# The opening of a fused Fourier and gated-cosine kernel: a first step without seed, two stores moved, and constant products around the second stage

## The chip, the cores and the metric

The kernel runs on one core of a Trainium2 chip. Five engines work side by side: PE (TensorE, matrix products), DVE (VectorE), ACT (ScalarE), POOL (GpSimd) and SP (SyncE), which here issues the transfers. The metric is device time of one execution in microseconds, the median over the runs shown. Everything is float32.

## The reference

```python
def _attn_ref(x):                       # x: (8, 3008, 256)
    X = np.fft.fft(x, axis=1)
    X = np.fft.fft(X, axis=2)
    return X.real.astype(np.float32)
...
def _moe_ref(x, w_in, w_out):           # (24064, 256), (256, 2048), (2048, 256)
    h = x @ w_in
    g = h * np.cos(h)
    return (g @ w_out).astype(np.float32)
```

The real part of a two-dimensional Fourier transform is fed, row by row, into two products with h times cos(h) between them.

## The kernel before, in words

The Fourier transform along the 256 columns is folded into `w_in`: `fold_weights` (L349) multiplies `w_in` by cosines and sines and gives WC and WS, in four quarters of 512 columns. `take_wn` (L362) takes the first row of a quarter of WS out into the columns of `wn`, and POOL then clears that row, because the row belongs to a column of another symmetry. The transform along the 3008 rows has two stages, 47 times 64. In the first (`fold` L210, `first_half` L231) VectorE or POOL folds a chunk of x, PE multiplies it by a table into `pz`, and ScalarE copies it to `zs`. There are eight chunks for a batch. `store_z` (L266) writes a chunk's `zs` to DRAM and `load_z` (L278) reads it back in another order as `z2`. Both can do a part of the columns, 0 to 4 of 24 or 4 to 24. The second stage (`second_half` L290) multiplies four blocks of `z2` by the table BJ into `pb`, and ScalarE copies the result to `pq`: one group of up to 256 columns, 225 in group 0. There are 6 groups in each of 8 batches.

A group passes through 8 steps of the network, 384 steps in all. A step fills a bank `H` with a seed (`seed` L418, ScalarE: 0.25 plus one row `nb` times a column of `wn`), adds products with WC (`mm1` with 0, L432), copies twice that to `ew` (`act_e`), adds products with WS (`mm1` with 1), and takes `h` as the difference on VectorE (`dve_h`). So one pair of products serves two mirrored sets of rows. Then follow rounding, sine, and the combinations for the second product (`mm2` L507, into banks `M`, seven products instead of eight). `nb` is one row of `pq` spread over 128 partitions: for the first group by a product with a row of ones into `pn` (L317 to L321), for the others by a trip through DRAM (L323 to L325).

The order of the program is written by hand, and every engine runs its own instructions in that order; all transfers are issued by SP in order. Ahead of the steps stands the opening (L640 to L696): first `keep_busy` (L392), products of a constant tile VX that nobody reads; then the eight chunks of batch 0 interleaved with three quarters of the weights; the small parts of the stores (columns 0 to 4) before the first read of z (L681); `fold_quarter(2)`, two constant products (L684); then the last weights, the other parts of the stores of chunks 4 to 7, further constants, the second read of z, and `second_half(0, 0)`. The rest of chunks 2 and 3 is stored ahead of the first read (L674, L675). Then comes `seed(steps[0])` (L721) and the loop over steps (L722), in which step 0 is followed at once by `fold_weights(1, 3)`. The dictionary `opening` (L697) places what is left over into steps 0 to 22, such as `fold_weights(0, 3)`, `take_wn(3)`, VectorE's sums of `w_out` (`combine_w2` L406) and the other groups of batch 0. Steps 3 and later of each batch carry the first stage of the next one, in which POOL folds.

The banks of PSUM are shared: `H` has three, `M` four, and the second stage one.

Of the kernel before, what the change touches and what calls it, by code (L numbers as in the profile page):

```python
# [11 lines left out]
FP = mybir.dt.float32  # L12
# [69 lines left out]
def _width(g):  # L82
    return 225 if g == 0 else 256
# [24 lines left out]
def kernel(  # L108
# [7 lines left out]
    nc = tc.nc  # L116
# [10 lines left out]
    cpool = ctx.enter_context(tc.tile_pool(name="consts", bufs=1))  # L127
# [50 lines left out]
    def load_bj(c0, c1):  # L178
        nc.sync.dma_start(out=BJ[:, c0:c1], in_=B_dr.ap()[:, c0:c1])
# [21 lines left out]
    def psum(name, tag="fft"):  # L201
        return ppool.tile([128, 512], FP, tag=tag, bufs=bank[tag], name=name)
# [63 lines left out]
    def store_z(b, c, j0=0, j1=NJ):  # L266
        half, q = divmod(c, NCH // 2)
        if q == 0 and j0 == 0:
            zds[b, half] = dpool.tile([32, 2 * NJ * 128], FP, tag="zd", bufs=4, name="zd")
        zd, zs = zds[b, half], zss[b, c]  # L270
        for e in range(2):
            p0 = 16 * e + IP * q
            nc.sync.dma_start(
                out=zd[p0 : p0 + IP, 256 * j0 : 256 * j1].rearrange("i (y d) -> y i d", d=128),
                in_=zs[64 * e + 2 * j0 : 64 * e + 2 * j1, :].rearrange("y (i d) -> y i d", d=128),
            )
# [11 lines left out]
    ready = {}  # L288

    def second_half(b, g):  # L290

        T = _width(g)
        z2 = z2s[b]
        pb = psum("pb")
        for q in range(4):
            jj = 4 * g + q
            nc.tensor.matmul(  # L297
                pb[:, 128 * q : 128 * q + 128],
                lhsT=z2[:, jj * 128 : jj * 128 + 128],
                rhs=BJ[:, jj * 128 : jj * 128 + 128],  # L300
                start=True,
                stop=True,
            )
        pq = spool.tile([128, 512], FP, tag="pq", bufs=8, name="pq")
        pv = pq[:, 0 : 2 * T].rearrange("d (e t) -> d e t", e=2)
        bv = pb.rearrange("d (q e k) -> d e q k", q=4, e=2)
        if g == 0:
            nc.scalar.copy(
                out=pv[:, :, 0:192].rearrange("d e (q k) -> d e q k", k=64), in_=bv[:, :, 1:4, :]
            )  # L310
            nc.scalar.copy(out=pv[:, :, 192:225], in_=bv[:, :, 0, 0:33])
        else:
            nc.scalar.copy(out=pv.rearrange("d e (q k) -> d e q k", k=64), in_=bv)
        nb = spool.tile([128, 256], FP, tag="nb", bufs=8, name="nb")
        ready[b, g] = (pq, nb)
        if b == 0 and g == 0:
            pn = psum("pn", "M")  # L317
            nc.tensor.matmul(
                pn[:, 0:T], lhsT=ones, rhs=pq[0:1, T : 2 * T], start=True, stop=True
            )  # L320
            nc.scalar.copy(out=nb[:, 0:T], in_=pn[:, 0:T])  # L321
            return
        nd = dpool.tile([1, 256], FP, tag="nd", bufs=4, name="nd")  # L323
        nc.sync.dma_start(out=nd[:, 0:T], in_=pq[0:1, T : 2 * T])
        nc.sync.dma_start(out=nb[:, 0:T], in_=nd[0:1, 0:T].to_broadcast([128, T]))  # L325


    def transform(b):
        todo = {}
# [19 lines left out]
    def fold_weights(e, n, tag="M"):  # L349
        W = WS if e else WC  # L350
        pw = psum("pw", tag)
        for i in range(2):
            nc.tensor.matmul(  # L353
                pw,
                lhsT=CS[i][:, 128 * e : 128 * e + 128],
                rhs=wr[n // 2][i][:, 512 * (n % 2) : 512 * (n % 2) + 512],
                start=(i == 0),
                stop=(i == 1),
            )
        nc.scalar.copy(out=W[:, 512 * n : 512 * n + 512], in_=pw)  # L360

    def take_wn(n):  # L362
        row = WS[0:1, 512 * n : 512 * n + 512]
        pw = psum("pw", "M")
        for k in range(4):
            nc.tensor.matmul(
                pw[:, k : k + 1],
                lhsT=row[:, 128 * k : 128 * k + 128],
                rhs=ones[:, 0:1],
                start=True,  # L370
                stop=True,
            )
        nc.scalar.copy(out=wn[:, 4 * n : 4 * n + 4], in_=pw[:, 0:4])
        nc.gpsimd.memset(row, 0.0)

    def fold_quarter(n):
        fold_weights(1, n)
        fold_weights(0, n)
        take_wn(n)
# [6 lines left out]
    ones = cpool.tile([1, 128], FP, tag="ones", name="ones")  # L386
    nc.vector.memset(VX[:, 0:512], 1.0)
    nc.vector.memset(ones, 1.0)
    scratch = cpool.tile([1, 128], FP, tag="scratch", name="scratch")
    nc.scalar.activation(out=scratch, in_=ones, func=AF.Sin, bias=0.0, scale=SIN_SCALE / 8)  # L390

    def keep_busy(k, tag, n):  # L392
        pd = psum("pd", tag)
        for i in range(k):
            nc.tensor.matmul(
                pd[:, 0:n],
                lhsT=VX[:, 0:128],
                rhs=VX[:, 0:n],
                start=i == 0,
                stop=i == k - 1,  # L400
            )
# [16 lines left out]
    def seed(s):  # L418
        T = s.T
        s.pq, s.nb = ready[s.b, s.grp]  # L420
        s.H = psum("H", "H")
        for u in range(2):
            f = 2 * s.fp + u
            nc.scalar.activation(  # L424
                out=s.H[:, u * T : u * T + T],
                in_=s.nb[:, 0:T],
                func=AF.Copy,
                bias=0.25,
                scale=wn[:, f : f + 1],
            )  # L430

    def mm1(s, e):  # L432
        T = s.T
        W = WS if e else WC
        for u in range(2):
            f = 2 * s.fp + u
            nc.tensor.matmul(  # L437
                s.H[:, u * T : u * T + T],
                lhsT=W[:, 128 * f : 128 * f + 128],
                rhs=s.pq[:, e * T : e * T + T],  # L440
                start=False,
                stop=True,
                skip_group_check=True,
            )

    def act_e(s):
        s.ew = spool.tile([128, 512], FP, tag="ew", bufs=2, name="ew")
        nc.scalar.mul(out=s.ew[:, 0 : 2 * s.T], in_=s.H[:, 0 : 2 * s.T], mul=2.0)  # L448
# [187 lines left out]
    def chunk(c):  # L636
        fold(0, c, 0)
        fold(0, c, 1)
# [32 lines left out]
    first_half(0, 5)  # L671
    store_z(0, 4, 0, 4)
    store_z(0, 5, 0, 4)
    store_z(0, 2, 4)  # L674
    store_z(0, 3, 4)  # L675
    chunk(7)
    first_half(0, 6)
    first_half(0, 7)
# [2 lines left out]
    for half in range(2):  # L681
        load_z(0, half, 0, 4)
    fold_quarter(2)
    keep_busy(2, "M", 256)  # L684
    load_w(3)
    load_w2(0, 2)
    load_w2(2, 4)
    for c in range(4, 8):
        store_z(0, c, 4)
    load_bj(512, 1024)  # L690
    for half in range(2):
# [1 line left out]
    load_w2(4, 6)  # L693
    load_w2(6, 8)
    load_bj(1024, NJ * 128)
    second_half(0, 0)  # L696
    opening = {  # L697
        0: ((fold_weights, 0, 3), (take_wn, 3), (combine_w2, 0, 2)),
        1: ((combine_w2, 2, 4),),
# [7 lines left out]
    steps = []  # L707
    for b in range(NB):
        for g in range(NG):
            for fp in range(8):  # L710
                s = Step()
# [3 lines left out]
    n = len(steps)  # L715

    def step(t, last=None):
        s = steps[t] if 0 <= t < n else None
        return s if s is not None and (last is None or s.fp == 7) else None

    seed(steps[0])  # L721
    for t in range(n + LAG + 1):  # L722
        cur, prev, old, done = step(t), step(t - 1), step(t - 2), step(t - LAG)
        if cur:
            if t % per == 0:
                todo = transform(cur.b + 1) if cur.b + 1 < NB else {}
            mm1(cur, 0)
            act_e(cur)
            if t == 0:
                fold_weights(1, 3)  # L730
        if t - LAG - 1 == n - 1:
            combine_last(steps[n - 1])
            break
        if step(t - LAG - 1, True):
            take_m(step(t - LAG - 1), 1)
            combine_m(step(t - LAG - 1))
        if done:
            mm2(done, 0)
        if old:
            dve_g(old, 0)  # L740
            dve_g(old, 1)
        if step(t + 1):
            seed(step(t + 1))
        if prev:
            dve_frac(prev, 0)
        if old:
            dve_s(old, 0)
        if prev:
            dve_frac(prev, 1)
            act_sin(prev)  # L750
        if old:
            dve_s(old, 1)
        if step(t - LAG, True):
            take_m(done, 0)
        if cur:
            mm1(cur, 1)
        if done:
            mm2(done, 1)
        if cur:
            dve_h(cur)  # L760
            act_round(cur, 0)
            act_round(cur, 1)
        if old:
            dve_s(old, 2)
        if step(t - LAG - 2, True):
            store_out(step(t - LAG - 2), 0)
        if step(t - LAG - 3, True):
            store_out(step(t - LAG - 3), 1)
        for call in opening.pop(t, ()):
            call[0](*call[1:])  # L770
        for call in todo.pop(t % per, ()):
            call[0](*call[1:])
# [30 lines left out]
```

## Time and profile before

| what | value |
|---|---|
| median of three runs | 1977.77 us |
| the three runs | 1979.92, 1977.70, 1977.77 us |
| profiled execution, own time | 1979.79 us |
| its span, first to last instruction | 1978.0 us |
| mean granted TensorE clock | 0.996 |
| transfers | 88.63 MB, mean 45 GB/s |

The page of the profile gives busy time by engine, the chain that ended last, and the costliest groups of instructions. A row of the timeline has start, length, engine, line, operation, output and inputs, and in brackets the idle time before it with what ended that. PEld is the loading of weights for PE. A float32 product shows as two matmul instructions. The granted clock is a share of full speed.

### The profile page before, as it was taken

Reading aid. Unit: us, or ns where it says so; the run is one execution under the profiler, and the core shown is the slowest. Engines: PE = TensorE matmul, PEld = TensorE weight load, DVE = VectorE, ACT = ScalarE, POOL = GpSimd, SP = SyncE. Lnnn points to the kernel's source line nnn. Section 1 sums busy time; section 2 is a strip of 40 time slices with the busy share of each in tenths; the row PEclk is TensorE's granted clock in tenths of the full one; section 3 lists DMA queues with packets and bytes.
Section 4 is the critical chain, followed back from the end, with each engine's and each line's share of the span. In section 5 each row is a group of like instructions: output and inputs, shape, how many; then the busy total and the mean of one; then the engine's idle time right before and its main releaser. Section 6 shows DMA issues by size and latency. Waiting matters only on the chain.

```text
span 1978.0 us, 28633 instructions
## 1 busy us (share of the span) xinstructions
PE 1953.2 (99%) x9350; PEld 1704.2 (86%) x9350; DVE 1854.5 (94%) x3208; ACT 1483.8 (75%) x2688; POOL 465.4 (24%) x428
## 2 busy tenths in 40 slices
PE   8999999999999999999999999999999999999998
PEld 4888899888988889888898888988889888898887
DVE  2999989999899998999989999999999999899998
ACT  3777777777777778777877777777777777778775
POOL 1132212331133211323122222123311223112111
PEclk8999999999999999999999999999999999999999
DMA  8423121131112212122122311222022220200000
GB/s 199 91 43 58 31 52 37 35 64 35 43 31 42 57 35 43 36 49 50 32 42 42 67 26 36 44 55 55 19 41 51 47 51 20 47 21 10 18 16 22
DMA packets 176682, 88.63 MB, mean 45 GB/s; under 512 B 103303, under 2 KB 173622, under 8 KB 174902
## 3 DMA queue, kind: packets, MB, share of 16 engines
q1 hardware_dynamic: 176374, 86.68, 21.3%
q8 instruction: 75, 1.23, 0.3%
q14 instruction: 73, 0.60, 0.1%
q10 hardware_dynamic: 160, 0.13, 0.0%
HBM read 49.50 MB, written 37.27 MB: 44 GB/s over the span
## 4 chain that ended last, share of the span: by engine, by line
PE 91%; DVE 5%; ACT 1%; issue 1%; DMA 1%; SPq 0%; POOL 0%; DVEq 0%; ACTq 0%; POOLq 0%
PE M L529 53%; PE H L437 31%; PE pz L244 3%; PE pb L297 2%; DVE r L482 1%; DVE S L500 1%; DVE S L493 1%; PE pw L353 1%; DVE S L502 1%; DVE h L453 1%; DVE r L472 1%; ACT r L468 0%; DMA out_dram<-ob 0%; SPq L631 0%; DVE ob L621 0%
## 5 line engine op out<-in xcount | busy, mean ns | idle before, releaser
L478 ACT ACTIVATE r<-r 128x1024 f32<-128x1024 f32 (+1 forms) x384 | 398.5, 1038 | 306.4 <-DVE r L472 305.5
L529 PE MATMUL M<-S,VX 128*128 128x256 f32 (+1 forms) x2304 | 612.6, 375 | 0.0
L529 PEld LDWEIGHTS M<-S,VX 128*128 128x128 f32 x2304 | 438.1, 190 | 50.0
L437 PE MATMUL H<-pq,WS 128*128 128x256 f32 (+1 forms) x1536 | 390.5, 377 | 10.3 <-ACT ew L448 10.0
L437 PE MATMUL H<-pq,WC 128*128 128x256 f32 (+1 forms) x1536 | 395.0, 380 | 1.9 <-ACT H L424 1.9
L529 PE MATMUL M<-r,w 128*128 128x256 f32 (+1 forms) x1536 | 388.5, 375 | 0.0
L424 ACT ACTIVATE H<-nb,wn 128x256 f32<-128x256 f32 (+1 forms) x768 | 364.0, 474 | 17.3 <-DVE r L482 4.7
L453 DVE TENSOR_TENSOR h<-ew,H 128x512 f32<-128x512 f32 (+1 forms) x384 | 257.2, 670 | 98.1 <-PE H L437 89.3
L437 PEld LDWEIGHTS H<-pq,WS 128*128 128x128 f32 x1536 | 289.6, 190 | 53.5 <-ACT ew L448 18.9
L529 PEld LDWEIGHTS M<-r,w 128*128 128x128 f32 x1536 | 301.2, 197 | 27.2
L472 DVE SCALAR_TENSOR_TENSOR r<-r,h 128x512 f32<-128x512 f32 (+1 forms) x384 | 310.1, 808 | 0.0
L437 PEld LDWEIGHTS H<-pq,WC 128*128 128x128 f32 x1536 | 283.7, 190 | 30.7 <-ACT H L424 2.8
L218 POOL TENSOR_TENSOR xf<-xp 94x508 f32<-94x508 f32 x112 | 165.3, 1495 | 566.3 <-PE pz L251 553.8
L493 DVE TENSOR_TENSOR S<-r 128x512 f32<-128x512 f32 (+1 forms) x384 | 291.4, 759 | 0.1
L482 DVE SCALAR_TENSOR_TENSOR r<-h,r 128x512 f32<-128x512 f32 (+1 forms) x384 | 274.2, 714 | 0.0
L468 ACT ACTIVATE r<-H 128x512 f32<-128x512 f32 (+1 forms) x384 | 223.2, 581 | 56.0 <-DVE h L453 53.3
L448 ACT ACTIVATE ew<-H 128x512 f32<-128x512 f32 (+1 forms) x384 | 225.5, 587 | 48.7 <-PE H L437 44.4
L472 DVE SCALAR_TENSOR_TENSOR r<-r,H 128x512 f32<-128x512 f32 (+1 forms) x384 | 255.7, 666 | 0.0
L482 DVE SCALAR_TENSOR_TENSOR r<-H,r 128x512 f32<-128x512 f32 (+1 forms) x384 | 254.5, 663 | 0.3 <-ACT r L478 0.3
L468 ACT ACTIVATE r<-h 128x512 f32<-128x512 f32 (+1 forms) x384 | 236.1, 615 | 0.0
L529 PE MATMUL M<-r,VX 128*128 128x256 f32 (+1 forms) x768 | 225.5, 375 | 0.0
L529 PE MATMUL M<-S,w 128*128 128x256 f32 (+1 forms) x768 | 225.2, 375 | 0.0
(68 smaller groups left out, 1499.7 us busy)
## 6 DMA issues: line engine op xcount, KB each, us to landing
out_dram<-ob SPq DMA_DIRECT2D x728, 32.0 KB
xp<-in_x_dram SPq DMA_DIRECT2D x56, 256.0 KB
zd<-zs SPq DMA_DIRECT2D x112, 96.0 KB
z<-zd SPq DMA_DIRECT2D x28, 384.0 KB
xp<-in_x_dram SPq DMA_DIRECT2D x56, 120.0 KB
nb<-nd SPq DMA_DIRECT2D x40, 128.0 KB
wr<-in_moe_w_in_dram SPq DMA_DIRECT2D x8, 256.0 KB
w<-in_moe_w_out_dram SPq DMA_DIRECT2D x4, 512.0 KB
```

What stands on the lines that cost most here:

```text
L218: (nc.gpsimd if b else nc.vector).tensor_tensor(out=fv[:, e, :, 1:128], in0=xv[:, :, 1:128], in1=xv[:, :, 255:128:-1], op=ALU.subtract if ...
L244: nc.tensor.matmul(pz[rows, a:512], lhsT=w, rhs=fv[:, e, a:512], start=True, stop=True)
L424: nc.scalar.activation(out=s.H[:, u * T : u * T + T], in_=s.nb[:, 0:T], func=AF.Copy, bias=0.25, scale=wn[:, f : f + 1],)
L437: nc.tensor.matmul(s.H[:, u * T : u * T + T], lhsT=W[:, 128 * f : 128 * f + 128], rhs=s.pq[:, e * T : e * T + T], start=False, stop=True, ...
L448: nc.scalar.mul(out=s.ew[:, 0 : 2 * s.T], in_=s.H[:, 0 : 2 * s.T], mul=2.0)
L453: nc.vector.tensor_tensor(out=s.h[:, 0 : 2 * T].rearrange("p (u t) -> p u t", u=2)[:, :, ::-1], in0=s.ew[:, 0 : 2 * T].rearrange("p (u t) ...
L468: nc.scalar.activation(out=r, in_=h, func=AF.Copy, bias=BIG, scale=1.0)
L472: nc.vector.scalar_tensor_tensor(out=r, in0=r, scalar=-BIG, in1=h, op0=ALU.add, op1=ALU.subtract)
L478: nc.scalar.activation(out=r, in_=r, func=AF.Sin, bias=0.0, scale=SIN_SCALE)
L482: nc.vector.scalar_tensor_tensor(out=r, in0=h, scalar=-0.25, in1=r, op0=ALU.add, op1=ALU.mult)
L493: nc.vector.tensor_tensor(out=sv[:, 0:2], in0=gv[:, 2:3].to_broadcast([128, 2, T]), in1=gv[:, 0:4:3], op=ALU.subtract,)
L529: nc.tensor.matmul(acc[key][m // 2][:, 256 * (m % 2) : 256 * (m % 2) + T], lhsT=w, rhs=a, start=first, stop=s.fp == 7, skip_group_check=True,)
```

## The change

The first step gets no seed from ScalarE. Its bank is filled with 0.25 by VectorE ahead of the second stage, and the row's part is added by two products with one row each (`seed_first`): the row of `wn` as it stood in WS, kept in a new tile `wrow`, times the row of `pq`. The row `nb`, still needed from step 1 on, is spread behind the first products and their copy (`spread_nb`). The rest of chunks 2 and 3 is stored behind the first read of z, ahead of that of chunks 4 to 7. One more constant product stands before the second stage (three, not two), and two stand behind it.

```diff
@@ second_half, first group of batch 0
-            pn = psum("pn", "M")
-            nc.tensor.matmul(
-                pn[:, 0:T], lhsT=ones, rhs=pq[0:1, T : 2 * T], start=True, stop=True
-            )
-            nc.scalar.copy(out=nb[:, 0:T], in_=pn[:, 0:T])
             return
...
+    def spread_nb():
+        pq, nb = ready[0, 0]
+        T = _width(0)
+        pn = psum("pn", "M")
+        nc.tensor.matmul(pn[:, 0:T], lhsT=ones, rhs=pq[0:1, T : 2 * T], start=True, stop=True)
+        nc.scalar.copy(out=nb[:, 0:T], in_=pn[:, 0:T])
@@ take_wn
         nc.scalar.copy(out=wn[:, 4 * n : 4 * n + 4], in_=pw[:, 0:4])
+        if n == 0:
+            nc.scalar.copy(out=wrow, in_=row[:, 0:256])
         nc.gpsimd.memset(row, 0.0)
...
+    wrow = cpool.tile([1, 256], FP, tag="wrow", name="wrow")
...
+    def seed_first(s):
+        for u in range(2):
+            nc.tensor.matmul(
+                s.H[:, u * s.T : u * s.T + s.T],
+                lhsT=wrow[:, 128 * u : 128 * u + 128],
+                rhs=s.pq[0:1, s.T : 2 * s.T],
+                start=False,
+                stop=True,
+                skip_group_check=True,
+            )
@@ the opening
     store_z(0, 5, 0, 4)
-    store_z(0, 2, 4)
-    store_z(0, 3, 4)
     chunk(7)
...
     fold_quarter(2)
-    keep_busy(2, "M", 256)
+    keep_busy(3, "M", 256)
     load_w(3)
     load_w2(0, 2)
     load_w2(2, 4)
-    for c in range(4, 8):
+    for c in range(2, 8):
         store_z(0, c, 4)
...
-    second_half(0, 0)
     opening = {
...
-    seed(steps[0])
+    first = steps[0]
+    first.H = psum("H", "H")
+    nc.vector.memset(first.H[:, 0 : 2 * first.T], 0.25)
+    second_half(0, 0)
+    keep_busy(2, "M", 256)
+    first.pq, first.nb = ready[0, 0]
     for t in range(n + LAG + 1):
...
             mm1(cur, 0)
+            if t == 0:
+                seed_first(cur)
             act_e(cur)
             if t == 0:
+                spread_nb()
                 fold_weights(1, 3)
```

## The prediction

> **What bounds the kernel now.** I read the page first, then the chain of waits in the window where the work changes, then the granted clock there, and last the timeline of single engines.
>
> ```profile
> span 1978.0 us, 28633 instructions
> PE 1953.2 (99%) x9350; PEld 1704.2 (86%) x9350; DVE 1854.5 (94%) x3208; ACT 1483.8 (75%) x2688; POOL 465.4 (24%) x428
> PE 91%; DVE 5%; ACT 1%; issue 1%; DMA 1%; SPq 0%; POOL 0%; DVEq 0%; ACTq 0%; POOLq 0%
> ```
>
> PE is busy for 1953.2 of 1978.0 us and holds 91% of the chain. The change touches no instruction of the 384 steps but the first. It can only shift the time at which the steps start, so the question is how many us the opening loses and whether the rest follows. The chain through the opening:
>
> ```profile
> 34.47 2.03 DMA z<-zd
> ...
> 36.64 1.63 PE pb L297 x8
> 38.30 0.49 ACT pq L308
> 38.81 0.23 ACT pq L311
> 39.08 1.13 PE pn L318 x2
> 40.23 0.36 ACT nb L321
> 40.61 0.46 ACT H L424
> 41.09 0.46 ACT H L424
> 41.60 1.87 PE H L437 x4
> 43.47 3.41 PE pw L353 x4
> 46.88 1.06 PE H L437 x4
> 47.94 1.72 PE pw L353 x4
> ```
>
> Columns are start, length, what. The reader is to see two things. From 39.08 to 41.60 nothing but the spreading of one row (pn, nb) and the seeds of step 0 is on the path. And four products of L353 take 3.41 us at 43.47 but 1.72 at 47.94. The second is the clock, in the table of windows (after the busy times come the granted clock, the DMA share and GB/s):
>
> ```profile
> 36.00:37.00 1.00, 0.36 (x3) 0.39 (x4) 0.00 (x0) 0.00 (x0) 0.00 (x0) 1.00 0.73 101
> 37.00:38.00 1.00, 1.00 (x7) 0.96 (x6) 0.00 (x0) 0.00 (x0) 0.00 (x0) 0.56 0.81 277
> ...
> 40.00:41.00 1.00, 0.19 (x1) 0.00 (x0) 0.00 (x0) 0.74 (x2) 0.00 (x0) 0.50 1.06 365
> 41.00:42.00 1.00, 0.40 (x1) 0.41 (x2) 0.00 (x0) 0.51 (x2) 0.00 (x0) 0.50 0.80 265
> ```
>
> The clock is halved in the 37th us, right behind PE's gap ahead of pb, and by the lengths of L353 it is full again shortly before 47.94.
>
> Does a shift reach the end? Behind the opening VectorE is the bound for some 50 us, then PE:
>
> ```profile
> 48.04 0.62 DVE L453 TENSOR_TENSOR h<-ew,H 128x450 f32<-128x450 f32 x1 [19.40 <-PE H L437]
> 80.00:100.00 20.00, 19.38 (x106) 17.48 (x105) 20.00 (x36) 15.83 (x31) 3.71 (x5) 1.00 0.14 24
> 100.00:120.00 20.00, 20.00 (x98) 17.15 (x97) 19.79 (x33) 14.98 (x29) 7.77 (x7) 1.00 0.15 34
> ```
>
> VectorE is full from 80 to 100, PE from 100 on; both regimes begin with VectorE's first h, at 48.04, which waited for PE. If that moves and no transfer is late for it, the end moves by as much.
>
> **The change part by part.** I follow the path to that first h.
>
> *Start of the second stage.* It needs z and a free PE. The stores:
>
> ```profile
> 29.75 0.27 SPq L273 DMA_DIRECT2D zd<-zs x1
> 30.91 0.40 SPq L273 DMA_DIRECT2D zd<-zs x1
> 32.48 0.31 SPq L273 DMA_DIRECT2D zd<-zs x1
> 29.87 0.59 ACT L260 COPY zs<-pz 128x512 f32<-128x512 f32 x1 [0.61 <-PE pz L251]
> 34.37 1.13 PE L395 MATMUL pd<-VX 128*128 128x256 f32 x4
> 36.64 1.62 PE L297 MATMUL pb<-BJ,z 128*128 128x128 f32 x8 [1.14 <-DMA z<-zd]
> ```
>
> By their place in the program, the four issues from 29.75 to 30.91 are the moved stores; the stores of chunks 6 and 7 follow, the last at 32.48. Without the four, chunk 6 goes at 29.75, and chunk 7 when its copy ends (29.87 + 0.59 = 30.46), its last issue at about 30.9. The last read of z then goes at 34.47 - 1.6 = 32.9 and z is there at 34.9 instead of 36.5. But the third constant product is now in front: two pairs took 1.13, and a third adds half of that without the fill. L353's row below gives 3.70 / 8 = 0.46 for one 512-column pass, so two 256-column passes add 0.46. PE is free at 34.37 + 1.13 + 0.46 = 35.96, so about 1 us of the earlier z is not used. pb starts at 35.9 (I let it overlap the drain), **0.75** sooner.
>
> *Clock.* With that product and two more behind pb, PE has no gap above some 0.1 us from 29.76 on, so I take it at full clock through the opening. Rows at full clock:
>
> ```profile
> 29.76 3.70 PE L353 MATMUL pw<-wr,CS 128*128 128x512 f32 x8
> 71.98 1.05 PE L297 MATMUL pb<-BJ,z 128*128 128x128 f32 x8
> 62.98 0.92 PE L437 MATMUL H<-pq,WC 128*128 128x225 f32 x4
> 63.74 0.93 PE L529 MATMUL M<-r,w 128*128 128x225 f32 x4
> ```
>
> pb ends at 35.9 + 1.05 = 36.95 (now 38.27). Next on PE came 39.08 - 38.27 = 0.81 after pb, for the two copies of pq; that gives 37.76. The two new constant products last 1.13 less a drain, about 0.9, so to 37.85: they hide beside the copies and cost 0.1. At half clock they would need 1.8 and cost 1.0.
>
> *Removed:* pn, nb and two seeds ahead of the first products: 41.60 - 39.08 = **2.52**.
>
> *Added on PE:* the first products at full clock pass in 0.76 (62.98 to 63.74, start to start), the one-row products have as many columns and passes. No row shows them; bounds are 0.76 (same spacing) and 1.13 (two pn at full clock, 1.13 / 2 each, not overlapped). I take 0.76, as they are queued back to back. The spreading of the row (pn) now stands in front of L353: half of 0.76, 0.38 (bound 0.57). Then L353 1.72 and the second products 0.92.
>
> **Sum:** 37.85 + 0.76 + 0.76 + 0.38 + 1.72 + 0.92 = 42.39, against 47.94 now (46.88 + 1.06): **5.55 us earlier**. The clock's part is pb 0.58, pn 0.57, first products 0.95, L353 1.69, second 0.14: 3.9. The other 1.65 is order.
>
> *Costed at nothing.* The constant fill of H, on VectorE, falls in its 19.40 us of idleness. The copy of wrow (like nb, 0.36) makes POOL's clearing of that row 0.4 us later, near 16.3, and with it POOL's next fold copy and perhaps the chunk after it; the bound is 0.5 us, and a wait for x further on covers it:
>
> ```profile
> 26.99 1.81 PE L244 MATMUL pz<-xf,L 128*64 128x512 f32 x5 [1.38 <-POOL xf L225]
> 54.02 0.33 SPq L149 DMA_DIRECT2D xp<-in_x_dram x1
> SPq L149 <- DMA z<-zd: 1.5, 1, 1.5
> 58.00:60.00 2.00, 2.00 (x6) 1.78 (x6) 2.00 (x6) 1.84 (x4) 0.00 (x0) 0.50 1.03 194
> 62.51 0.62 DVE L453 TENSOR_TENSOR h<-ew,H 128x450 f32<-128x450 f32 x1 [0.26 <-PE M L529]
> ```
>
> Step 1's seeds need nb; ScalarE makes it at 40 and the seeds after L353's copy near 42, ahead of their products at 44.8. *The moved stores* sit on SP ahead of the constants' and z's second load. That z landed by 54.0 (SP's wait for it ended there) and is first used at 71.98, 66.4 after the change: four issues of up to 0.75 us, less the 1.6 us earlier start, leave 10 us of room. The weights behind the first z come 1.6 us sooner: their fast stretch ends near 41.2 (365 GB/s, then 265), 39.6 after, the half of w2 for VectorE's sums at 42.9 earlier still.
>
> *The second fall of the clock* (58 to 60) stays, as the gaps around it move along. It cost VectorE 0.26 us. [...]
>
> The profiled execution took 1979.79 us (span 1978.0): 1979.79 - 5.55 = **1974.2**. The runs shown lie at two levels, 1977.70 and 1977.77, and 1979.92; the profiled one is of the upper. I take the 2.1 us between them as clock: full rather than half speed for 4 us more in the opening. A kernel with no low stretch has one level, and 1974.2 stands for it: 3.6 under the median (0.18%), 5.6 under the upper level.
>
> [...]
>
> **The rivals.**
>
> *The levels are not the opening's clock* (0.18). Then all 5.55 comes off the median: 1972.2. For it: nothing profiled shows a run of the lower level. Against: no other place of this trace has a low clock for long.
>
> *The clock falls anyway* (0.13), through products that don't count as activity or gaps elsewhere (the one-column products just before 34.37 are nearly idle). Only the 1.65 of order is left: 1977.77 - 1.65 = 1976.1. For it: products stood back to back from 41.60, and L353 from 43.47 to 46.88 was still slow: the clock rises late. Against: it need not rise here, only stay, and the constant products are full passes as L353's, under which it stood at 1.00.
>
> *z is not earlier* (0.07): the stores of chunks 6 and 7 or the read land at 36.5 for another reason than the queue. pb starts at 36.64, 0.75 is lost: 1975.0.
>
> *Slower: the clock is low before the constant products start* (0.08). Place: PE from 34.4 on. Three products take 2.5 and end at 37.1, pb 1.63 (38.75), two products 1.8 (40.5), first and one-row products 1.5 each (43.5), pn 0.75, L353 3.41, second products 1.5 (49.2), L353 3.41 again, 52.6 against 49.66 now: 2.9 later, 1982.7. It decides if the clock falls by 34.4, before the last product of the weights is done; what speaks for it is PE's 1.38 us wait at 26.99, against it the clock of 1.00 until 37.
>
> **How the numbers follow.** Forecast 1974.2 with chance 0.54, spread 1973.3 to 1975.2 by the bounds above (one-row products and pn up to 0.56 dearer, second fall -0.26 to +0.75, pb's start 0.3). About 0.2% of 1977.77, 3.96 us, is what a measurement of this kernel can tell from no change; that is 1973.8. Of the forecast 0.24 lies beyond it and 0.30 within. Faster: 0.24 + 0.18 = 0.42. Same: 0.30 + 0.13 + 0.07 = 0.50. Slower: 0.08. The range 1972.2 to 1976.2 takes in all but the slower rival and part of the edges.
>
> **What would show it.** Right: granted clock 1.00 from 29 to about 46; pb starting near 35.9 straight behind pd; mm1 (L437) of step 0 near 37.9; h near 42.5; PE's next steps 5.5 us earlier to the end. Wrong: a clock of 0.50 before 46, pb waiting for z, VectorE's L414 waiting for w2, PE waiting for z at the second pb, or a first h at 42.5 with a later loss (VectorE beside POOL's folds, or a longer second fall).

## The result, and the profile after

The changed kernel took 1974.46 us (median of 13 runs, 1973.65 to 1975.57), against 1979.83 for the kernel before in as many (1977.70 to 1981.32). The ratio is 0.9975, with a 95% interval from 0.9968 to 0.9983: 0.25% faster. That is clear of no change, but not quite of the 0.2% that the prediction called the limit of what can be told, since the interval reaches down to 0.17%. The forecast time was 1974.2. What it had too low is the kernel before: its three runs had a median of 1977.77, thirteen have 1979.83.

The page of the changed kernel answers to the lines shown of before. Its profiled execution took 1974.87 us.

```profile
span 1973.1 us, 28657 instructions
PE 1948.9 (99%) x9360; PEld 1702.4 (86%) x9360; DVE 1854.4 (94%) x3209; ACT 1482.7 (75%) x2687; POOL 465.1 (24%) x428
PE 91%; DVE 5%; DMA 2%; ACT 1%; issue 1%; SPq 0%; DVEq 0%; POOL 0%; ACTq 0%; POOLq 0%
```

The span is 4.9 us shorter, with nearly the same work on every engine. (PE has ten matmul instructions more, and its busy time still falls by 4.3 us, since those of the opening run at full clock.) The chain of waits through the opening, start, length, what; L400 is `keep_busy`, L453 `mm1`, L439 the one-row products, L355 `fold_weights`:

```profile
35.20 1.49 PE pd L400 x6
36.69 0.89 PE pb L297 x8
37.59 0.86 PE pd L400 x4
38.45 0.98 PE H L453 x4
39.43 0.95 PE H L439 x4
40.38 0.38 PE pn L327 x2
40.76 1.91 PE pw L355 x4
42.68 0.76 PE H L453 x4
```

Where the chain of before went from SP over a transfer to PE, and from there twice to ScalarE and back, it now stays on PE. No wait for z is left in it. The same table of windows as before, with the granted clock third from the end:

```profile
37.00:38.00 1.00, 1.00 (x9) 0.95 (x8) 0.00 (x0) 0.38 (x1) 0.00 (x0) 1.00 0.90 254
40.00:41.00 1.00, 1.00 (x6) 0.70 (x5) 0.00 (x0) 0.58 (x2) 0.00 (x0) 1.00 1.02 355
46.00:47.00 1.00, 1.00 (x6) 0.72 (x5) 0.71 (x2) 0.16 (x1) 0.51 (x1) 1.00 0.94 323
```

It is 1.00 where it was 0.50. Two more rows of VectorE's timeline set the measure for everything below: the fold of chunk 6, which waits for the last fourth of x, and the first h.

```profile
26.92 1.28 DVE L218 TENSOR_TENSOR xf<-xp 94x508 f32<-94x508 f32 x2 [0.92 <-DMA xp<-in_x_dram]
43.55 0.62 DVE L469 TENSOR_TENSOR h<-ew,H 128x450 f32<-128x450 f32 x1 [13.62 <-PE H L453]
```

In the kernel before that fold began earlier, and the first h later (48.04, shown with the prediction):

```profile
26.16 2.48 DVE L218 TENSOR_TENSOR xf<-xp 94x508 f32<-94x508 f32 x4 [1.74 <-DMA wr<-in_moe_w_in_dram]
```

The bracket of this row names a load of weights, as brackets are inferred. The semaphores of the trace show the last load of x itself: it landed at 26.04, and at 26.80 in the changed kernel. In all ten profiles of the table below that landing lies 0.12 to 0.13 us ahead of the fold, whatever the bracket names.

So x arrived 0.76 us later in the profiled execution of the changed kernel, and the first h still came 4.49 us sooner. From the fold to the first h it is 21.88 us before and 16.63 after: 5.25 us gained, with x's arrival taken out.

### The profile page after: what moved, and what is told of

The parts are those of the page before. It is cut to its first block, busy times and chain, and to the rows that moved or that the text cites. A ratio compares the mean times of both kernels' runs of the same rounds, so it can differ in the third digit from the quotient of the medians.

```text
span 1973.1 us, 28657 instructions
## 1 busy us (share of the span) xinstructions
PE 1948.9 (99%) x9360; PEld 1702.4 (86%) x9360; DVE 1854.4 (94%) x3209; ACT 1482.7 (75%) x2687; POOL 465.1 (24%) x428
## 4 chain that ended last, share of the span: by engine, by line
PE 91%; DVE 5%; DMA 2%; ACT 1%; issue 1%; SPq 0%; DVEq 0%; POOL 0%; ACTq 0%; POOLq 0%
PE M L545 53%; PE H L453 31%; PE pz L244 3%; PE pb L297 2%; DVE r L498 1%; DMA xp<-in_x_dram 1%; DVE S L516 1%; DVE S L509 1%; DVE S L518 1%; DVE h L469 1%; DVE r L488 1%; ACT r L484 0%; PE pw L355 0%; DMA out_dram<-ob 0%; SPq L647 0%
## 5 line engine op out<-in xcount | busy, mean ns | idle before, releaser
L453 PE MATMUL H<-pq,WS 128*128 128x256 f32 (+1 forms) x1536 | 390.2, 376 | 11.5 <-ACT ew L464 11.2
L453 PE MATMUL H<-pq,WC 128*128 128x256 f32 (+1 forms) x1536 | 393.9, 379 | 0.5 <-ACT H L429 0.5
L453 PEld LDWEIGHTS H<-pq,WS 128*128 128x128 f32 x1536 | 289.3, 190 | 53.9 <-ACT ew L464 20.0
L453 PEld LDWEIGHTS H<-pq,WC 128*128 128x128 f32 x1536 | 283.2, 190 | 28.9 <-ACT H L429 0.8
```

The source lines that it names most:

```text
L453: nc.tensor.matmul(s.H[:, u * T : u * T + T], lhsT=W[:, 128 * f : 128 * f + 128], rhs=s.pq[:, e * T : e * T + T], start=False, stop=True, ...
```

## The experiments

Twelve runs were made, in four sets of kernels on one chip each; the kernel before ran beside each set (medians 1979.44, 1979.13, 1978.95 and 1979.20). One table holds what the profiles of the first two sets have in common, beside those of before and of the changed kernel: the start of chunk 6's fold, the start of pb in the timeline, the first h, the difference of fold and h, and what is left from the first h to the end of that execution's own time.

| kernel | fold | pb | first h | fold to h | own time | h to end | median |
|---|---|---|---|---|---|---|---|
| before | 26.16 | 36.64 | 48.04 | 21.88 | 1979.79 | 1931.75 | 1979.83 |
| changed | 26.92 | 36.53 | 43.55 | 16.63 | 1974.87 | 1931.32 | 1974.46 |
| products only (e1) | 26.52 | 38.26 | 48.24 | 21.72 | 1979.20 | 1930.96 | 1976.61 |
| no products (e2) | 26.72 | 36.82 | 48.50 | 21.78 | 1979.33 | 1930.83 | 1977.74 |
| none behind (e3) | 27.68 | 37.63 | 44.72 | 17.04 | 1976.37 | 1931.65 | 1975.80 |
| seed on ScalarE (e6) | 26.19 | 35.80 | 43.33 | 17.14 | 1975.22 | 1931.89 | 1975.22 |
| changed again (c) | 26.80 | 36.41 | 43.42 | 16.62 | 1974.82 | 1931.40 | 1974.34 |
| two ahead (e4) | 25.55 | 34.76 | 41.85 | 16.30 | 1973.90 | 1932.05 | 1973.90 |
| stores back (e5) | 26.33 | 36.95 | 44.04 | 17.71 | 1975.43 | 1931.39 | 1975.86 |
| late clear (e7) | 26.56 | 36.16 | 43.18 | 16.62 | 1974.57 | 1931.39 | 1974.33 |

The column ahead of the last carries the argument: whatever is done to the opening, the end follows the first h by 1930.8 to 1932.1 us.

### The constant products alone (e1)

```diff
 kernel before
-    keep_busy(2, "M", 256)
+    keep_busy(3, "M", 256)
...
     second_half(0, 0)
+    keep_busy(2, "M", 256)
```

> The kernel before with the constant products alone (three ahead of the second stage, two behind the spreading of the row); order of stores and seed as before. My theory (the products hold the clock): granted clock 1.00 through the opening, the clock's 3.9 us are gained, the third product costs nothing since z lands later than it ends: 3.9 us under the kernel before. Rival (the clock falls anyway, products that nobody needs do not hold it): clock 0.50 from about 37 us, no gain, within 0.5 us of the kernel before.

Measured: 1976.61 (11 runs, 1975.45 to 1979.20), ratio 0.9985 (0.9976 to 0.9994). Eight runs lie from 1975.45 to 1976.96, three from 1978.36 to 1979.20. The profiled one is of the upper three. Its row of pb in the timeline, and its windows:

```profile
38.26 1.13 PE L297 MATMUL pb<-BJ,z 128*128 128x128 f32 x8 [1.97 <-DMA z<-zd]
...
39.00:40.00 1.00, 0.39 (x4) 0.19 (x2) 0.00 (x0) 0.55 (x2) 0.00 (x0) 0.77 0.85 282
40.00:41.00 1.00, 0.80 (x2) 0.49 (x2) 0.00 (x0) 0.15 (x1) 0.00 (x0) 0.50 0.88 263
```

Here z came late, PE waited 1.97 us behind its three products, and the clock fell, for 6.8 us (10.2 in the kernel before). So the products gain 2.8 us in the median (3.9 were expected), but on their own they do not hold the clock in every execution: with the stores in front, the wait for z can outlast them. That the eight faster runs kept the clock is likely but not shown, as none of them was profiled.

### No constant products (e2)

```diff
 changed kernel
-    keep_busy(3, "M", 256)
...
     second_half(0, 0)
-    keep_busy(2, "M", 256)
```

> The changed kernel without any constant product around the second stage. My theory: PE is idle or nearly idle for about 2 us ahead of the second stage (one-column products, then the wait for z), the clock falls there and the first products and the weights run at half speed; pb itself starts up to 0.4 us sooner. Some 3 to 3.5 us slower than the changed kernel, clock 0.50 in the opening. Rival (with the seeds off the path the gaps are too short for the clock to fall): clock 1.00, 0 to 0.5 us faster than the changed kernel.

Measured: 1977.74 (11 runs from 1973.44 to 1980.07), ratio 0.9984 (0.9975 to 0.9993). The chain of waits in the profiled run:

```profile
36.82 1.14 PE pb L297 x8
...
38.77 1.87 PE H L453 x4
40.63 1.79 PE H L439 x4
42.43 0.75 PE pn L327 x2
43.18 3.71 PE pw L355 x4
```

The first products take 1.87 and the weights 3.71, as in the kernel before, and the one-row products 1.79 instead of 0.95: the clock fell behind a wait for z of 1.82 us, and the order of seed and stores alone is left. The runs spread over 6.6 us, and the mean granted clock over the whole run orders them: the two runs with 0.999 took 1973.44 and 1974.60, the five with 0.996 or less 1977.74 to 1980.07. So without the products it differs by execution whether the clock falls. In the thirteen runs of the changed kernel the mean clock is 0.998 or 0.999. The median is 3.3 us over the changed kernel, as my theory had it. The best run lies 0.2 us under the best of the changed kernel, which would fit the rival (a sooner start of pb where the clock stays), but no such run was profiled.

### None behind the second stage (e3)

```diff
 changed kernel
     second_half(0, 0)
-    keep_busy(2, "M", 256)
```

> The changed kernel with the three products ahead of the second stage and none behind it: one gap of about 0.8 us on PE, beside the two copies of pq. My theory: too short, the clock stays at 1.00, first products start up to 0.1 us sooner, time within 0.3 us of the changed kernel. Rival (the two products behind are what holds the clock): clock 0.50 from 38 us on, 2 to 3 us slower than the changed kernel.

Measured: 1975.80 (10 runs, 1974.35 to 1977.09), ratio 0.9979 (0.9969 to 0.9988). The windows around the gap of 0.81 us that is left beside the copies of pq, and those of a later stage:

```profile
39.00:40.00 1.00, 0.42 (x2) 0.42 (x3) 0.00 (x0) 0.50 (x2) 0.00 (x0) 1.00 0.89 273
40.00:41.00 1.00, 1.00 (x6) 0.71 (x5) 0.00 (x0) 0.00 (x0) 0.00 (x0) 1.00 1.02 341
...
55.00:56.00 1.00, 1.00 (x4) 0.91 (x3) 1.00 (x4) 1.00 (x2) 0.00 (x0) 0.50 1.13 221
```

The clock stays at 1.00 in the opening, so the two products behind pb are not what held it here. The median is 1.3 us over the changed kernel, more than the expected 0.3, though not the 2 to 3 of the rival. In this profile x arrived 0.8 us later than in the changed kernel's, PE waited 0.18 us for z, and the second fall of the clock came at 54. How much of the 1.3 is due to the missing products, and not to these, the runs don't settle.

### Seed on ScalarE (e6)

```diff
 changed kernel, second_half
         if b == 0 and g == 0:
+            pn = psum("pn", "M")
+            nc.tensor.matmul(
+                pn[:, 0:T], lhsT=ones, rhs=pq[0:1, T : 2 * T], start=True, stop=True
+            )
+            nc.scalar.copy(out=nb[:, 0:T], in_=pn[:, 0:T])
             return
 take_wn
-        if n == 0:
-            nc.scalar.copy(out=wrow, in_=row[:, 0:256])
 and the opening
...
-    nc.vector.memset(first.H[:, 0 : 2 * first.T], 0.25)
...
+    seed(steps[0])
...
-                seed_first(cur)
...
-                spread_nb()
```

> The changed kernel with the row spread and step 0 seeded on ScalarE ahead of the first products, as in the kernel before; stores and constant products as changed. My theory (order of seed is worth what full-clock rows give): pn, nb and seeds take about 2.0 us on the path, the one-row products and the later pn 1.1 us less, so 0.9 to 1.0 us slower than the changed kernel, clock 1.00. Rival (the stall of the seeds is what lets the clock fall): clock 0.50, 3 to 4 us slower than the changed kernel.

Measured: 1975.22 (9 runs, 1973.87 to 1976.35), ratio 0.9975 (0.9965 to 0.9985). The chain of waits:

```profile
37.67 0.66 PE pn L318 x2
38.33 0.02 issue
38.35 0.36 ACT nb L321
...
39.72 1.03 PE H L456 x4
40.75 1.72 PE pw L360 x4
42.46 0.76 PE H L456 x4
```

Spreading and seeds take 39.72 - 37.67 = 2.05 us, as expected at full clock. But the one-row products that replace them take 0.95 where 0.76 was reckoned, and the later pn 0.38 and a slower start of the weights (1.91 for 1.72) come on top. Fold to h is 17.14 against 16.62: the step without seed is worth 0.5 us in the profile, half of what was expected. The medians differ by 0.8, which is not clear of the spread of the runs. The clock was 1.00 throughout the opening, so PE's waits of 0.82 and 0.35 us for the copies and seeds did not make it fall here, with products around them.

### The changed kernel again (c), and the stores put back (e5)

> The changed kernel once more, beside the next three on the same chip, as their yardstick. In the six profiles so far the time from the first h of step 0 to the end is 1930.8 to 1931.9 us, whatever the kernel, and the start of chunk 6's fold, which waits for x, varies from 26.2 to 27.7. My theory: the time is the start of that fold, plus 16.6 us to the first h, plus some 1931.4. So 1974 to 1976. Rival (the spread is the clock): a low stretch in the opening in some executions.

Measured: 1974.34 (7 runs, 1973.81 to 1974.82), ratio 0.9973 (0.9962 to 0.9984); fold to h 16.62, as in the first profile to 0.01 us, and the clock 1.00 to the last steps.

```diff
 changed kernel
     store_z(0, 5, 0, 4)
+    store_z(0, 2, 4)
+    store_z(0, 3, 4)
...
-    for c in range(2, 8):
+    for c in range(4, 8):
         store_z(0, c, 4)
```

> The changed kernel with the rest of chunks 2 and 3 stored ahead of the read of z, as before. My theory: z lands 1.0 to 1.6 us later, PE waits for it behind the third product; 0.8 to 1.3 us slower where the clock stays, and in some executions that wait lets the clock fall as with the products alone (then 4 us slower); median 1 to 2 us slower. Rival (the moved stores were not what the read of z waited for): within 0.3 us.

Measured: 1975.86 (11 runs, 1975.41 to 1977.97), 1.5 us over the changed kernel beside it; ratio 0.9985 (0.9976 to 0.9994). PE waits for z again:

```profile
36.95 1.13 PE L297 MATMUL pb<-BJ,z 128*128 128x128 f32 x8 [0.85 <-DMA z<-zd]
```

Fold to h is 17.71, 1.09 us more. The clock stayed at 1.00 behind this wait of 0.85 us, and no run of the eleven lost 4 us. The read of z did wait for the moved stores.

### Two products ahead (e4, e11), and with the fold on VectorE (e10)

```diff
 changed kernel
-    keep_busy(3, "M", 256)
+    keep_busy(2, "M", 256)
```

> The changed kernel with two constant products ahead of the second stage, as before, and two behind. My theory now: z lands about when the third product ends (without the ones behind, PE waited 0.18 us for z), so taking one away makes PE wait for z instead: at most 0.3 us faster, clock 1.00. Rival (the prediction's step, z is there 1 us before the third product ends): 0.4 to 0.5 us faster.

> Two constant products ahead once more. My theory: PE does not wait for z, pb is 0.3 to 0.4 us sooner after chunk 6's fold than in the changed kernel, median 0.3 to 0.4 us under its 1974.34 to 1974.46, which is about the spread between calls. Rival: z is late in some executions and the gain is gone.

Measured: 1973.90 (6 runs) and 1974.21 (9 runs), ratios 0.9971 (0.9960 to 0.9983) and 0.9976 (0.9967 to 0.9986). The first profile:

```profile
33.75 1.13 PE L400 MATMUL pd<-VX 128*128 128x256 f32 x4
34.76 1.13 PE L297 MATMUL pb<-BJ,z 128*128 128x128 f32 x8
```

pb follows the products without a wait, against my theory of that run, but only just. By the semaphores z landed 0.14 us ahead of pb (0.13 in the second run), which is the lag with which pb follows z where PE does wait for it (34.47 + 2.03 = 36.50 against 36.64 in the kernel before). With three products z landed at 36.00 and they ended at 36.69. So z is there 0.7 us ahead of the third product's end, not the 1 us of the prediction's step, and just in time for two. Fold to h is 16.30 and, in the second, 16.43: 0.2 to 0.3 us less than with three, not the 0.4 to 0.5 of the rival. The medians are 0.1 to 0.6 us lower than the changed kernel's two, within the spread between sets; that this beats the changed kernel is not shown.

The last kernel adds to it batch 1's first fold on VectorE:

```diff
-        (nc.gpsimd if b else nc.vector).tensor_tensor(
+        (nc.gpsimd if b and (b, c) != (1, 0) else nc.vector).tensor_tensor(
```

> Two constant products ahead of the second stage, and batch 1's first fold on VectorE instead of POOL (same work, other engine, at its place behind step 6). VectorE pays two folds of about 0.62 us and loses no 1.4 to 2.1 us to POOL beside it. My theory: 0.2 to 0.8 us faster than two ahead alone, so 1973.1 to 1973.7. Rival (POOL's later folds come sooner into VectorE's stage and collide there): no gain, 1973.9 or more.

Measured: 1974.52 (10 runs, 1973.18 to 1975.81), beside 1974.21 in the same set. No gain in the median, as the rival had it. VectorE's own two folds took 1.27 us, and the collision described next, which they replace, costs 1.4 to 2.1. What takes up the rest the runs don't show: POOL's next folds started at 82.94, 0.62 us sooner than in e11 (83.56), which speaks for the rival but is no proof.

### Clearing later (e7)

```diff
 take_wn
-        nc.gpsimd.memset(row, 0.0)
+        if n:
+            nc.gpsimd.memset(row, 0.0)
...
     chunk(3)
+    nc.gpsimd.memset(WS[0:1, 0:512], 0.0)
```

> The changed kernel with the first cleared row of WS cleared behind the fold copy of chunk 3 on POOL, so that the copy of wrow holds up no fold. My theory: the product of chunk 3 starts some 0.5 us sooner, and PE waits as much longer for x further on: within 0.3 us of the changed kernel. Rival (the delay is carried to the second stage): 0.5 to 0.7 us faster.

Measured: 1974.33 (7 runs), beside 1974.34; ratio 0.9971 (0.9960 to 0.9982). The clear that waits for wrow costs nothing that can be seen, as the prediction had it.

### POOL's first fold cut to a sliver (e8)

The changed kernel's first h is not followed at a constant distance: the h of step 6 comes 28.67 us after the first in c, but 29.32 in e4 and 28.13 in e1. The rows between, of c, first POOL's fold of batch 1, then VectorE:

```profile
64.86 2.92 POOL L218 TENSOR_TENSOR xf<-xp 94x508 f32<-94x508 f32 x2 [18.21 <-DMA xp<-in_x_dram]
...
65.93 0.72 DVE L518 TENSOR_TENSOR S<-r,S 128x225 f32<-128x225 f32 x1
66.57 1.82 DVE L419 TENSOR_TENSOR VX<-w 128x256 f32<-128x256 f32 x2
```

The same rows of e4:

```profile
64.22 2.64 POOL L218 TENSOR_TENSOR xf<-xp 94x508 f32<-94x508 f32 x2 [19.15 <-DMA xp<-in_x_dram]
...
64.36 1.38 DVE L518 TENSOR_TENSOR S<-r,S 128x225 f32<-128x225 f32 x1
65.66 1.82 DVE L419 TENSOR_TENSOR VX<-w 128x256 f32<-128x256 f32 x2
```

The fold starts when batch 1's x lands, at a time that does not follow the first h (63.70 in the kernel before with the first h at 48.04, 64.86 in c with 43.42), and some of VectorE's instructions beside it are stretched (not the h of step 5, which took its 0.62 us in c). To see whether that reaches the end, most of the fold was left out:

```diff
 changed kernel, fold
+        w = 4 if (b, c) == (1, 0) else 128
-            out=fv[:, e, :, 1:128],
-            in0=xv[:, :, 1:128],
-            in1=xv[:, :, 255:128:-1],
+            out=fv[:, e, :, 1:w],
+            in0=xv[:, :, 1:w],
+            in1=xv[:, :, 255 : 256 - w : -1],
...
     first_half(0, 7)
+    early.append(spool.tile([128, 2 * IP * 128], FP, tag="xf", bufs=1, name="xf"))
+    nc.gpsimd.memset(early[0][0:94], 0.0)
```

> The changed kernel with POOL's fold of batch 1's first chunk cut from 127 columns to 3 (the rest of that chunk is zero, so most of that fold is left out; POOL fills the tile early, while VectorE is idle). In the changed kernel that fold starts at 64.9, when x lands, and beside it VectorE's instructions stretch by 1.4 us (L518 0.72 for 0.39, the pair of L419 1.82 for 0.75). My theory: VectorE bounds there, so the h of step 6 comes 1.2 to 1.4 us sooner after the first h and the end with it. Rival (PE or a wait takes its place): at most 0.3 us.

Measured: 1973.26 (7 runs, 1972.27 to 1973.94), ratio 0.9972 (0.9961 to 0.9983). The rows:

```profile
64.40 0.38 POOL L221 TENSOR_TENSOR xf<-xp 94x12 f32<-94x12 f32 x2 [18.78 <-DMA xp<-in_x_dram]
...
64.90 0.39 DVE L521 TENSOR_TENSOR S<-r,S 128x225 f32<-128x225 f32 x1
65.20 0.75 DVE L422 TENSOR_TENSOR VX<-w 128x256 f32<-128x256 f32 x2
```

The same two instructions take 0.39 and 0.75. The h of step 6 comes 27.26 us after the first, 1.41 sooner, and the end 1929.88 after it, 1.5 sooner. In these profiles the collision reaches the end in full; the medians, from different chips, differ by 1.1 us.

### Without the last load of x (e9)

```diff
-    load_x(0, 3)
+    take_x(0, 3)
 fold
-        xv = xs[b, c // 2].rearrange
+        xv = xs[b, 2 if (b, c // 2) == (0, 3) else c // 2].rearrange
```

> The changed kernel without the load of the last fourth of batch 0's x; chunks 6 and 7 are folded from the third fourth, so that load is left out. My theory: in the opening PE waits only for x, so chunk 6's fold starts 1 to 1.5 us sooner (near 25.3), the first h stays 16.6 us behind it, and the time falls by as much less what the collision on VectorE costs more (1.4 to 2.1 us by its place), with a spread under 1 us. Rival (the stores or the read of z, or the weights, take x's place): first h no sooner than 43.

Measured: 1972.69 (6 runs, 1972.42 to 1973.28), ratio 0.9970 (0.9958 to 0.9981). VectorE folds four chunks in one go:

```profile
22.10 4.98 DVE L218 TENSOR_TENSOR xf<-xp 94x508 f32<-94x508 f32 x8 [4.67 <-DMA xp<-in_x_dram]
...
41.22 0.62 DVE L469 TENSOR_TENSOR h<-ew,H 128x450 f32<-128x450 f32 x1 [13.62 <-PE H L453]
```

Chunk 6's fold, the fifth of the eight instructions, begins at 24.57, and the first h is 41.22 - 24.57 = 16.65 behind it. That is 2.2 us sooner than in c (43.42), of which 1.65 reach the end in the medians. The collision takes a part of the rest: the h of step 6 comes 29.55 us after the first here, 28.67 in c. The six runs span 0.9 us, no less than the seven of c with 1.0, so that x makes the spread is not shown. That the arrival of the last x sets the opening where the clock is held is: without that wait the first h comes sooner by as much as the fold.

## Why the prediction was right, and where it was not

- **The clock.** Right, and the largest term. Held, the clock is 1.00 through the opening in all profiles with products and moved stores. With the products or the order undone (e2, e1), it falls in some executions. The kernel before shows it too: of 30 runs beside the first set, the twelve with a mean clock of 0.998 have a mean time of 1978.5, the eleven with 0.996 of 1981.0. The forecast's reading that the levels are clock stands as far as that goes; there are more than two of them. The size was too large for the median: 3.9 us is what the clock costs where it is low for 10.2 us, as in the profiled execution. In the medians the products alone gained 2.8 us (e1), and leaving them out cost 3.3 (e2).
- **Which level stands for before.** Here the step failed. Two of three runs shown were of the lower level, and the forecast took the median of them, 1977.77, as where the gain is counted from: 3.6 us, 0.18%. With more runs it is 1979.83 and the gain 5.4. The chances, 0.42 for faster and 0.50 for the same, were worked out from 1977.77 and lean to the same for that reason; counted from 1979.83, the forecast of 1974.2 would have lain beyond the 0.2%. The time did not hang on it, since it was worked out from the profiled execution.
- **Start of the second stage.** Right: 0.75 sooner was forecast, and from chunk 6's fold it is 10.48 us before (36.64 - 26.16) and 9.77 after (36.69 - 26.92, by the chain), 0.71 less (0.87 by the timeline, 36.53). That z is there before the third product ends holds in the changed kernel, by 0.7 us (36.00 against 36.69) where the prediction had 1.06, and once not (e3, where PE waited 0.18 us). With the stores put back (e5), PE waits for z behind the third product, and the profile loses 1.09 us.
- **From pb to the first products.** 0.90 forecast (36.95 to 37.85), 0.86 measured (37.59 to 38.45, by the chain).
- **First products to the second ones.** Mis-sized: 4.54 us was the sum of the five terms, 4.99 is measured (38.45 to 43.44). The one-row products took 0.95 (0.76 taken, bound 1.13), the first products 0.98 (0.76), the weights 1.91 (1.72), the second products 0.76 (0.92). Why the first products took longer than their spacing from start to start at full clock stays open.
- **Costed at nothing.** The late clear: right (e7). The fill of H: right, it lies at 29.5, ahead of the 13.62 us for which VectorE waits for the first h. The weights were in time: VectorE's first sum follows the first h without a wait.
- **The shift reaches the end.** Right, but for a term that was missing: the collision with POOL's fold. It was in the rows of before as well, yet its price depends on what it meets: added up over the stretched instructions, 1.07 us in e1, 1.4 in c, 2.06 in e4. The second fall of the clock did not stay, as the prediction had it: in the profile of the changed kernel the clock is 1.00 from the opening to the last steps. It fell there in e3, e6, e9 and e11, near 50 to 54 us. The spread of the forecast allows it -0.26 to +0.75 around a price of 0.26. That span was my estimate and no run shows it; the runs had 0 (c) and 0.30 (e3). The price was about right, 0.30 where it can be read without the collision: the h of step 4 comes 18.25 us after the first in e3, where it fell, and 17.95 in c, where it did not.
- **Why the sum came out.** The profiled execution gained 4.92 us (1979.79 to 1974.87) where 5.55 was forecast. x came 0.76 later, the five terms were 0.45 dearer, pb took 0.16 less (0.89 in the chain for 1.05), and the time from the first h to the end was 0.43 shorter, some 0.3 of it the second fall that did not come: 5.55 - 0.76 - 0.45 + 0.16 + 0.43 = 4.93. The largest of these errors is the arrival of x, which the prediction took as fixed. That the forecast of 1974.2 came within 0.3 us of the median is in part luck: the errors offset each other, and the profiled execution of the kernel before happened to lie at its usual level (1979.79 against a median of 1979.83).
- **The rivals.** The clock fell anyway in none of the profiles with the whole change. In e1 and e2 it fell behind waits of 1.97 and 1.82 us; behind 0.85 us (e5) it stayed. Low clock before the products start was seen in none. (The sum of that rival has a slip: 2.5 us from 34.4 end at 36.9, not 37.1, which makes 1982.5 of its 1982.7.) That z is not earlier is ruled out by e5. The first rival, that the levels are not the opening's clock, takes all 5.55 us off the median. Off the median of thirteen runs it was 5.4, but the mean clock orders the runs of the kernel before, as said above, which speaks against it.

## What to carry to other kernels

When an opening stalls PE, look at the granted clock in the us behind the stall: here about half of the gain (2.8 of 5.4 us in the medians, e1) came with the constant products alone. Products that nobody needs held it at 1.00 here where PE waited for z no more than 0.85 us behind them (the changed kernel, e3, e5); where it waited 1.97 us (e1) the clock fell to 0.50. So shorten that wait too, or the gap is only moved. And count a gain from enough runs of the kernel before: where the clock's fall differs by execution, three runs can all but miss its usual level.

## What the runs showed of the hardware

- The granted clock fell to 0.50 behind some waits of PE and stayed at 1.00 behind others, and the length of the single wait does not order them. It fell behind waits of 1.14 us in the kernel before, 1.97 in e1 and 1.82 in e2, all ahead of pb. It stayed behind 1.78 us in e3 (to 28.51), 1.45 in e1 (to 27.35) and 0.85 in e5. In the kernel before it was at 0.50 from 37.11 for 10.24 us, at 1.00 for 10.24, and at 0.50 from 57.59 for 3.41. In the 3.41 us ahead of the falls PE was busy for 2.27 us (37.11; 0.74 of them products of one column, L366) and 1.61 (57.59), in e1 for 1.28 and in e2 for 1.41. In the 3.41 us from 26.87 in e3, which hold most of the wait of 1.78 and behind which the clock stayed, it was busy for 1.77. Here are these stretches of before (the first), of e1 and of e3; PE's busy time is the second number, and the granted clock of the stretch itself stands third from the end:

```profile
33.70:37.11 3.41, 2.27 (x15) 1.83 (x15) 0.00 (x0) 0.55 (x2) 0.51 (x1) 1.00 0.49 109
...
36.14:39.55 3.41, 1.28 (x9) 0.97 (x8) 0.00 (x0) 0.13 (x1) 0.00 (x0) 1.00 0.57 142
...
26.87:30.28 3.41, 1.77 (x9) 0.91 (x10) 2.50 (x5) 0.57 (x2) 1.32 (x2) 1.00 0.80 229
```

  What decides whether the clock falls, and why e1 and e2 differ from run to run, no run shows.
- Beside POOL's fold of batch 1 some of VectorE's elementwise instructions took longer: 0.72 and 1.82 us in c (1.4 us more than the 0.39 and 0.75 of e8, beside 2.92 us of folds), 1.38 and 1.82 in e4 (2.06 more, beside 2.64). What it cost differed by what the fold met, 1.07 us in e1 to 2.06 in e4, and in e8 it was regained to the end.
- With the same loads ahead of it, x came at different times: chunk 6's fold began between 25.55 and 27.68 us in the ten profiles of the table, each time 0.12 to 0.13 us behind the landing of the last x. The first h, and the end with it, moves along.
- The one-row products took about as long as full ones of the same columns: 0.95 us beside 0.98 at a clock of 1.00 (the changed kernel), 1.79 beside 1.87 at 0.50 (e2).
